# An image and text attention block on one core: layer norm interleaved, scaling while leaving PSUM, a new order of v's parts, and another load order

## The chip, the cores and the metric

The kernel runs on one core of a Trainium2 chip. The metric is device time in microseconds for one execution; 125.17 us is the median of three runs before the change. The engines are named as in the profile: PE (matrix multiplication; PEld is its weight load), DVE (vector), ACT (scalar, activation functions), POOL (GpSimd) and SP (which issues transfers). PE writes into PSUM, eight banks of accumulators; DVE and ACT read it, POOL works on SBUF alone. Each engine runs its own queue in order and waits for others by semaphores.

## What is computed

Two batches of 256 image tokens and 32 text tokens, width D = 1152, all in bfloat16:

```python
mod_i = (_silu(c) @ wmod_img).reshape(B, 6, 1, D)
mod_t = (_silu(c) @ wmod_txt).reshape(B, 6, 1, D)
hi = _layernorm(x_img, axis=-1) * (1 + sci) + shi
ht = _layernorm(x_txt, axis=-1) * (1 + sct) + sht
qkvi = hi @ wqkv_img
qkvt = ht @ wqkv_txt
...
scores = jnp.einsum('bqd,bkd->bqk', q, k) * D ** (-0.5)
p = _softmax(scores, axis=-1)
a = jnp.einsum('bqk,bkd->bqd', p, v)
...
out_i = x_img + gai * (ai @ wo_img)
out_t = x_txt + gat * (at @ wo_txt)
```

`shi`, `sci`, `gai` (shift, scale, gate) are the first three of the six parts of `mod_i`, and `sht`, `sct`, `gat` those of `mod_t`. q, k and v join the text and the image rows.

## The kernel before

The order of the work on every engine is written out by hand: instructions go into each queue in the order of the program. The 512 image tokens are four tiles of 128 (0 and 1 are batch 0, 2 and 3 batch 1), and D is nine blocks of 128 (`kt`). `hT_i` holds the normalised image tokens transposed: D on the partitions, in nine blocks, tokens along the free axis.

**Loads.** All big loads are in SP's queue, in program order: token tiles 0 and 1, then chunk 0 of the scale weight `w_sc_i` and of v's weight `w_v_i` (`load_pair`), token tiles 2 and 3, the chunks 1 to 3 of that pair, the text tokens, the shift weight `w_sh_i`, q's weight `w_q_i` in three thirds. `KC` cuts the nine blocks into chunks of 2, 2, 2 and 3. Later loads (in `load_w`, L76) are text shift `w_sh_t`, text scale `w_sc_t`, image k `w_k_i`, and on to the output weights. Whole weights share six buffers (`wpool`); a seventh weight waits until a buffer's last reader is done.

**First stage (L214 to L307).** For each tile: statistics in three chunks of 384 (`ln_stats`, L143), their aggregate (L145), a square root on ACT (L147), then reciprocal and normalisation on DVE (`ln_apply`, L151, L152); nine PE transposes into two PSUM tiles of five and four blocks (`x_transposes`, L161), which ACT copies into `hT_i` (L162). The scale is computed chunk by chunk on PE (`mod_scale`, L169; from PSUM by ACT, L179, or DVE, L177), and multiplied into `hT_i` in place (`apply_mod`: DVE L187, POOL L190 or L192, ACT L194 or L196). `v_part(i, half, ch)` (L208) adds chunk `ch` to the accumulator of one half of v's columns (512) of token tile `i`; seven such accumulators stay open in PSUM. PSUM has seven banks for all of this (`ps_mm`) and one (`ps_sm`) for the modulation. v uses the scaled but not yet shifted tokens; its remaining columns follow in `v_rest` (L296) and L303.

**Shift.** `mod_cols` (L169) with `w_sh_i` gives the image shift; DVE copies it to `mod_i` (L309), ACT to `shT32` (L310), and `apply_mod` adds it to `hT_i` in place. What the shift adds to v is one row for each batch, computed from `shT32` by `mod_rows` (L334), sent to memory (L344), broadcast back (`bvb`, L350), and added by `v_shift` (L354). 

**q, k and the text.** `qk_img` (L378) makes q, then k, column block by column block: the first group has three blocks of 128 columns, then one by one, nine matmuls each. Calls can be hooked in ahead of a group. `txt_rows_shift` and `txt_rows_scale` make the text modulation as rows: 36 matmuls (L334), out of PSUM (ACT L137 or DVE L338), two writes to memory each by POOL (L344); after the scale, four loads by POOL broadcast both to the text tokens' partitions (`mb_t`, L392). `txt_modulate` (L400, L401, DVE) multiplies and adds, `txt_transposes` (L406 PE, L407 ACT) makes `hT_t`, and only then come the text's q and k (L418), the scores, the softmax, the product with v and the outputs.

Of the kernel before, what the change touches and what calls it, by code (L numbers as in the profile page):

```python
# [8 lines left out]
ACT = mybir.ActivationFunctionType  # L9
# [5 lines left out]
def kernel(  # L15
# [14 lines left out]
    nc = tc.nc  # L30
    bf = mybir.dt.bfloat16
    f32 = mybir.dt.float32
    PSUM = bass.MemoryType.PSUM

    B, NI, D = x_img.shape
# [101 lines left out]
            nc.scalar.copy(out_ap, in_ap)  # L137
        evac_idx[0] += 1

    def ln_stats(x_ap, np_):  # L140
        stats = small.tile([P, NCH, 6], f32, tag="stats")
        for k in range(NCH):
            nc.vector.bn_stats(stats[0:np_, k, :], x_ap[:, k * CH:(k + 1) * CH])  # L143
        mv = small.tile([P, 2], f32, tag="mv")
        nc.vector.bn_aggr(mv[0:np_, :], stats[0:np_, :, :])  # L145
        rstd = small.tile([P, 1], f32, tag="rstd")
        nc.scalar.activation(rstd[0:np_, :], mv[0:np_, 1:2], ACT.Sqrt, bias=eps_t[0:np_, :])  # L147
        return mv, rstd

    def ln_apply(x_ap, np_, out_ap, mv, rstd):  # L150
        nc.vector.reciprocal(rstd[0:np_, :], rstd[0:np_, :])  # L151
        nc.vector.tensor_scalar(out_ap, x_ap, mv[0:np_, 0:1], rstd[0:np_, :], op0=ALU.subtract, op1=ALU.mult)  # L152

    xn_i = act.tile([P, NIT, D], bf, tag="A")
    hT_i = act.tile([P, KT, B * NI], bf, tag="Bt")

    def x_transposes(i):
        for (k0, k1) in ((0, 5), (5, KT)):
            tp = ps_mm.tile([P, 5, P], bf, tag="mm")
            for kt in range(k0, k1):  # L160
                nc.tensor.transpose(tp[:, kt - k0, :], xn_i[:, i, kt * P:(kt + 1) * P], ident[:])  # L161
            nc.scalar.copy(hT_i[:, k0:k1, i * P:(i + 1) * P], tp[:, 0:k1 - k0, :])  # L162

    mod_i = const.tile([P, 2 * KT, B], f32, name="mod_img")

    def mod_cols(wt, out_ps, j0, j1):
        for j in range(j0, j1):
# [34 lines left out]
    def v_part(i, half, ch):  # L202
        k0, k1 = KC[ch]
        if ch == 0:
            vacc[i, half] = ps_mm.tile([P, VW], f32, tag="mm", name=f"va{i}{half}")
        ps = vacc[i, half]
        for kt in range(k0, k1):
            nc.tensor.matmul(ps[:], lhsT=hT_i[:, kt, i * P:(i + 1) * P], rhs=w_v_i[:, kt, half * VW:(half + 1) * VW],  # L208
                             start=(kt == 0), stop=(kt == KT - 1))
# [5 lines left out]
    st = ln_stats(x_i[:, 0, :], P)
    ln_apply(x_i[:, 0, :], P, xn_i[:, 0, :], *st)
    x_transposes(0)
    st = ln_stats(x_i[:, 1, :], P)
    mod_scale(0, "act")
    ln_apply(x_i[:, 1, :], P, xn_i[:, 1, :], *st)  # L220
    for kt in range(*KC[0]):
        apply_mod(kt, 0, 1, False, 1)
    x_transposes(1)
    for half in range(2):
        v_part(0, half, 0)
    st = ln_stats(x_i[:, 2, :], P)
    for kt in range(*KC[0]):
        apply_mod(kt, 1, 2, False, 1)
    ln_apply(x_i[:, 2, :], P, xn_i[:, 2, :], *st)
    mod_scale(1, "act")  # L230
    for half in range(2):
        v_part(1, half, 0)
    for kt in range(*KC[1]):
        apply_mod(kt, 0, 2, False, 1)
    x_transposes(2)
    st = ln_stats(x_i[:, 3, :], P)
    for kt in range(*KC[0]):
        apply_mod(kt, 2, 3, False, 1)
    ln_apply(x_i[:, 3, :], P, xn_i[:, 3, :], *st)
# [3 lines left out]
    x_transposes(3)
    for half in range(2):
        v_part(2, half, 0)
    for kt in range(*KC[0]):
        apply_mod(kt, 3, 4, False, 1)
    for kt in range(*KC[1]):
        apply_mod(kt, 2, 4, False, 0)
    mod_scale(2, "dve")  # L250
    for n, kt in enumerate(range(*KC[2])):
        apply_mod(kt, 0, 2, False, n % 2)
        apply_mod(kt, 2, 4, False, (n + 1) % 2)
    v_part(3, 0, 0)
    for half in range(2):
        v_part(2, half, 1)
    v_part(3, 0, 1)
# [12 lines left out]


    xn_t = act.tile([NTT, D], bf)
    st_t = ln_stats(x_t[:, :], NTT)
    ln_apply(x_t[:, :], NTT, xn_t[:, :], *st_t)
    junk = small.tile([P, 1], f32, bufs=1)
    nc.scalar.activation(junk[:], eps_t[:], ACT.Exp)
# [25 lines left out]
    for kt in range(KT):  # L302
        nc.tensor.matmul(ps[:], lhsT=hT_i[:, kt, 3 * P:4 * P], rhs=w_v_i[:, kt, VW:NM], start=(kt == 0), stop=(kt == KT - 1))  # L303
    evac(v_i[:, 3, VW:NM], ps[:])


    mps = ps_sm.tile([P, KT, B], f32, tag="sm")  # L307
# [1 line left out]
    nc.vector.tensor_copy(mod_i[:, 0:KT, :], mps[:])  # L309
    nc.scalar.copy(shT32[:, :, 0:B], mps[:])  # L310
    for kt in range(KT):
        apply_mod(kt, 0, TPB, True, (0, 1, 2, 0, 2, 1, 0, 0, 2)[kt])
    v_rest(TPB, NIT)

    w_sh_t = load_w(wmod_txt, 0)
    w_sc_t = load_w(wmod_txt, D)
    w_k_i = load_w(wqkv_img, D, K3)
    w_q_t = load_w(wqkv_txt, 0)
    w_k_t = load_w(wqkv_txt, D)
    w_ga_i = load_w(wmod_img, 2 * D)  # L320
# [22 lines left out]
        for b in range(B):  # L343
            nc.gpsimd.dma_start(gsc[si, b, :].rearrange("(g j) -> g j", g=NGG), g_sb[b:P:32, :])  # L344

    for kt in range(KT):
        apply_mod(kt, TPB, NIT, True, (0, 1, 2, 0, 2, 1, 0, 0, 2)[kt])
    mod_rows(w_v_i, 4, lhs=shT32)
    for b in range(B):
        nc.gpsimd.dma_start(bvb[:, b, :], gsc[4, b, :].partition_broadcast(P))  # L350
# [34 lines left out]
    def txt_rows_shift():  # L385
        mod_rows(w_sh_t, 0)
# [4 lines left out]
            for b in range(B):  # L391
                nc.gpsimd.dma_start(mb_t[b * NT:(b + 1) * NT, k, :], gsc[k, b, :].partition_broadcast(NT))  # L392

    qk_img(w_q_i, 0, hooks={5: v_shift, 6: txt_rows_shift})
    txt_rows_scale()

    hT_t = act.tile([P, KT, NTT], bf)

# [7 lines left out]
            nc.tensor.transpose(tpt[:, kt, :], xn_t[:, kt * P:(kt + 1) * P], ident[0:NTT, 0:NTT])  # L406
        nc.scalar.copy(hT_t[:], tpt[:])  # L407
# [227 lines left out]
```

## Time and profile before

| what | value |
|---|---|
| runs shown | 124.64, 125.17, 125.85 us |
| the profiled execution, first to last instruction | 124.3 us |
| PE busy | 110.7 us (89%) |
| DVE, ACT, POOL busy | 55.5, 31.6, 21.2 us |
| bytes moved, mean rate | 41.63 MB, 335 GB/s |

The page cuts the span into 40 slices of 3.1 us and gives each engine's busy share in tenths (9 is 90% or more), the granted PE clock, and the busy share of the transfer engines:

```profile
PE   0057999999999999999999999899999999999980
DVE  0778624146862120923022621134445656636680
ACT  4544052133572211110031121133524500012000
POOL 4005225160055030302430000002151000000000
PEclk9999999999999999999999999999999999999999
DMA  4999999999999999999999999999999997120231
```

PE starts in the third slice and is then busy to the end. The transfer engines are busy from the second slice to about 102 us. A row of the timeline gives start, length, engine, line, operation, the tile written and the tiles read, and the count of merged instructions; in square brackets stands the engine's idle time before it and what ended that. Matmuls overlap, so the length of a group is more than the sum of its steps; a step is the distance from one start to the next. A few matmul records are missing from the trace. In the chain of waits each piece has its start, its length and its line.

### The profile page before, as it was taken

The numbers are of one execution on the slowest core, as the hardware profiler recorded it, in microseconds if no ns is written. First come the engines' busy times: TensorE is split into PE (matmuls) and PEld (weight loads), VectorE is DVE, ScalarE is ACT, GpSimd is POOL, SyncE is SP. The second block draws the span as 40 slices with busy tenths as digits, with TensorE's granted clock in tenths as the row PEclk, the third lists the DMA queues.
The fourth block names the chain that finished last, engine by engine and source line by source line (L and its number), as shares of the span: only waits on it lengthen the run. The fifth ranks groups of instructions, "written<-read, shape, count | busy, mean of one in ns | idle before, by whom it ended". The sixth has DMA issues, their size and how long they took to land.

```text
span 124.3 us, 2647 instructions
## 1 busy us (share of the span) xinstructions
PE 110.7 (89%) x1126; PEld 65.8 (53%) x1134; DVE 55.5 (45%) x131; ACT 31.6 (25%) x72; POOL 21.2 (17%) x53
## 2 busy tenths in 40 slices
PE   0057999999999999999999999899999999999980
PEld 0044554546684444445444448777656555657650
DVE  0778624146862120923022621134445656636680
ACT  4544052133572211110031121133524500012000
POOL 4005225160055030302430000002151000000000
PEclk9999999999999999999999999999999999999999
DMA  4999999999999999999999999999999997120231
GB/s 107 267 348 376 377 383 350 348 414 413 408 406 413 397 414 422 406 406 412 404 383 402 381 409 411 407 411 405 411 405 417 371 411 299 61 95 0 100 96 49
DMA packets 22728, 41.63 MB, mean 335 GB/s; under 512 B 1148, under 2 KB 6428, under 8 KB 22716
## 3 DMA queue, kind: packets, MB, share of 16 engines
q1 hardware_dynamic: 21776, 39.74, 85.1%
q0 software_dynamic: 768, 1.64, 3.4%
q8 instruction: 9, 0.15, 0.4%
q10 hardware_dynamic: 171, 0.08, 0.2%
q14 instruction: 4, 0.02, 0.0%
HBM read 40.11 MB, written 1.35 MB: 333 GB/s over the span
## 4 chain that ended last, share of the span: by engine, by line
PE 85%; DVE 6%; ACT 4%; DMA 2%; issue 2%
PE qkps L378 28%; PE ps L568 13%; PE va L208 10%; PE gps L334 5%; PE ps L418 4%; PE aps L500 4%; PE sps L438 4%; PE mps L169 3%; ACT hT_i L162 2%; PE tp L161 2%; PE ps L587 2%; DMA c<-in_c_dram 2%; PE ps L515 2%; PE ps L296 2%; PE ps L303 2%
## 5 line engine op out<-in xcount | busy, mean ns | idle before, releaser
L378 PE MATMUL qkps<-hT_i,t 128*128 128x512 bf16 x157 | 35.4, 379 | 0.3
L378 PEld LDWEIGHTS <-t 128*128 128x128 bf16 x162 | 15.5, 98 | 18.9 <-issue 0.7
L568 PE MATMUL ps<-t,aT 128*128 128x384 bf16 (+2 forms) x117 | 18.1, 314 | 0.0
L208 PE MATMUL va<-w_v_i,hT_i 128*128 128x512 bf16 x60 | 16.0, 408 | 0.5 <-issue 0.2
L568 PEld LDWEIGHTS <-aT 128*128 128x128 bf16 x117 | 10.9, 98 | 6.8 <-issue 0.5
L571 DVE SCALAR_TENSOR_TENSOR tmp<-ps,rs,gb 128x384 bf16<-128x384 f32 (+2 forms) x13 | 7.6, 586 | 6.9 <-PE ps L568 6.9
L344 POOL DMA_DIRECT2D mod_scratch<-g_sb x8 | 4.8, 596 | 34.3 <-DVE g_sb L135 22.5
L208 PEld LDWEIGHTS <-hT_i 128*128 128x128 bf16 x63 | 6.2, 103 | 6.9 <-issue 1.5
L161 PE MATMUL tp<-ident,xn_i 128*128 128x128 bf16 x36 | 4.1, 287 | 5.4 <-DVE xn_i L152 5.4
L192 POOL TENSOR_SCALAR hT_i<-hT_i,mod_img 128x128 bf16<-128x128 bf16 (+1 forms) x14 | 6.1, 449 | 15.0 <-ACT mod_img L179 6.2
L362 DVE TENSOR_SCALAR qkT<-qkps 128x512 bf16<-128x512 f32 x5 | 3.4, 687 | 9.1 <-PE qkps L378 9.1
L137 ACT CAST qkT<-qkps 128x512 bf16<-128x512 f32 x5 | 2.8, 586 | 16.0 <-PE qkps L378 16.0
L161 PEld LDWEIGHTS <-xn_i 128*128 128x128 bf16 x36 | 3.3, 133 | 6.6 <-DVE xn_i L152 6.1
L135 DVE CAST qkT<-qkps 128x512 bf16<-128x512 f32 x4 | 2.8, 688 | 8.3 <-PE qkps L378 8.3
L162 ACT COPY hT_i<-tp 128x640 bf16<-128x640 bf16 (+1 forms) x8 | 4.7, 642 | 6.7 <-PE tp L161 6.7
L143 DVE BATCH_NORM_STATS2 stats<-x_i 128x6 f32<-128x384 bf16 x12 | 5.9, 546 | 0.0
L500 PE MATMUL aps<-pT,v_i 128*128 128x288 bf16 x36 | 5.4, 287 | 0.3 <-ACT pT L489 0.3
L418 PE MATMUL ps<-hT_t,t 128*128 128x64 bf16 x162 | 5.0, 193 | 0.5 <-issue 0.5
L418 PEld LDWEIGHTS <-t 128*128 128x128 bf16 x162 | 4.9, 98 | 0.9 <-issue 0.6
L364 ACT ACTIVATE qkT<-qkps 128x512 bf16<-128x512 f32 x4 | 2.3, 596 | 11.5 <-PE qkps L378 11.5
L334 PE MATMUL gps<-t,sT 128*32 128x288 bf16 x144 | 5.1, 287 | 0.0
L187 DVE TENSOR_SCALAR hT_i<-hT_i,mod_img 128x256 bf16<-128x256 bf16 x14 | 4.3, 368 | 1.5 <-ACT hT_i L162 1.3
(108 smaller groups left out, 119.0 us busy)
## 6 DMA issues: line engine op xcount, KB each, us to landing
t<-in_wmod_txt_dram SPq DMA_DIRECT2D x3, 2592.0 KB, 24.2
t<-in_wqkv_txt_dram SPq DMA_DIRECT2D x3, 2592.0 KB, 20.8
t<-in_wmod_img_dram SPq DMA_DIRECT2D x2, 2592.0 KB, 18.7
t<-in_wqkv_img_dram SPq DMA_DIRECT2D x6, 864.0 KB, 15.8
t<-in_wo_img_dram SPq DMA_DIRECT2D x1, 2592.0 KB, 22.1
t<-in_wo_txt_dram SPq DMA_DIRECT2D x1, 2592.0 KB, 24.3
w_sc_i<-in_wmod_img_dram SPq DMA_DIRECT2D x3, 576.0 KB, 7.8
w_v_i<-in_wqkv_img_dram SPq DMA_DIRECT2D x3, 576.0 KB, 7.9
```

The costliest lines, as they stand in the source:

```text
L143: nc.vector.bn_stats(stats[0:np_, k, :], x_ap[:, k * CH:(k + 1) * CH])
L161: nc.tensor.transpose(tp[:, kt - k0, :], xn_i[:, i, kt * P:(kt + 1) * P], ident[:])
L162: nc.scalar.copy(hT_i[:, k0:k1, i * P:(i + 1) * P], tp[:, 0:k1 - k0, :])
L192: nc.gpsimd.tensor_scalar(sl, sl, ap, 0.0, op0=ALU.mult, op1=ALU.add)
L208: nc.tensor.matmul(ps[:], lhsT=hT_i[:, kt, i * P:(i + 1) * P], rhs=w_v_i[:, kt, half * VW:(half + 1) * VW], start=(kt == 0), stop=(kt == K ...
L334: nc.tensor.matmul(gps[32 * g:32 * g + 32, :], lhsT=lhs[:, kt, :], rhs=w_blk[:, kt, g * VC:(g + 1) * VC], start=(kt == 0), stop=(kt == KT ...
L378: nc.tensor.matmul(pss[j - j0][:], lhsT=wq[:, kt, j * P:(j + 1) * P], rhs=hT_i[:, kt, :], start=(kt == 0), stop=(kt == KT - 1))
L418: nc.tensor.matmul(ps[:, j - j0, :], lhsT=wq[:, kt, j * P:(j + 1) * P], rhs=hT_t[:, kt, :], start=(kt == 0), stop=(kt == KT - 1))
L438: nc.tensor.matmul(sps[:], lhsT=qkT[:, ft, b, q0:q0 + P], rhs=qkT[:, KT + ft, b, :], start=(ft == 0), stop=(ft == KT - 1))
L500: nc.tensor.matmul(aps[:], lhsT=v_i[:, b * TPB + kj, dt * P:(dt + 1) * P], rhs=pTs[b][:, kj, :], start=(kj == 0), stop=False)
L568: nc.tensor.matmul(ps[:, 0:cw], lhsT=aT[:, dt, t0:t0 + P], rhs=w_o_i[:, dt, cs], start=(dt == 0), stop=(dt == KT - 1))
L571: nc.vector.scalar_tensor_tensor(tmp[:, 0:cw], ps[:, 0:cw], rsum[(b, qi)][:], gb[:, b, cs], op0=ALU.mult, op1=ALU.mult)
```

## The change

Five edits of order, and one of how the scale is applied.

1. `ln_stats` is split. The first statistics chunk of the next tile goes into DVE's queue ahead of the reciprocal and the normalisation of the tile before it; its other two chunks follow behind.
2. `x_transposes` only transposes. Its PSUM tile is emptied in parts: the first two blocks (four for tile 3) by ACT with the scale in the same instruction (`evac_scaled`), the others as plain copies (`evac_plain`). The steps of `apply_mod` for chunk 0 are gone, and that of chunk 1 for tile 3.
3. v's parts run in another order, with tile 0 and tile 1 chunk 0 together after tile 1's transposes.
4. `v_rest` for batch 1 moves ahead of the shift, and the shift is added to both batches block by block.
5. `w_k_i` is loaded ahead of `w_sh_t` and `w_sc_t`. The text modulation rows move out of the q pass into the k pass, behind its first three columns; `txt_modulate` and `txt_transposes` stand behind the k pass.

```diff
+    def evac_scaled(i, tps, n):
+        for kt in range(n):
+            nc.scalar.activation(hT_i[:, kt, i * P:(i + 1) * P], tps[0][:, kt, :], ACT.Identity,
+                                 scale=mod_i[:, KT + kt, i // TPB:i // TPB + 1])
+
+    def evac_plain(i, tps, n):
+        nc.scalar.copy(hT_i[:, n:5, i * P:(i + 1) * P], tps[0][:, n:5, :])
+        nc.scalar.copy(hT_i[:, 5:KT, i * P:(i + 1) * P], tps[1][:, 0:KT - 5, :])
...
+    def ln_next(i, first):
+        if first:
+            lns[i] = ln_stats(x_i[:, i, :], P, 0, 1)
+        else:
+            ln_stats(x_i[:, i, :], P, 1, NCH, lns[i])
+            lns[i] = ln_std(lns[i], P)
...
+    ln_next(0, True)
+    ln_next(0, False)
+    ln_next(1, True)
+    ln_out(0)
+    tps = x_transposes(0)
+    evac_plain(0, tps, 2)
+    ln_next(1, False)
+    ln_next(2, True)
+    ln_out(1)
     mod_scale(0, "act")
+    evac_scaled(0, tps, 2)
+    tps = x_transposes(1)
+    evac_scaled(1, tps, 2)
+    ln_next(2, False)
+    ln_next(3, True)
+    ln_out(2)
+    evac_plain(1, tps, 2)
+    for i in range(2):
+        for half in range(2):
+            v_part(i, half, 0)
+    tps = x_transposes(2)
+    evac_scaled(2, tps, 2)
+    ln_next(3, False)
+    ln_out(3)
     mod_scale(1, "act")
+    evac_plain(2, tps, 2)
     for kt in range(*KC[1]):
         apply_mod(kt, 0, 2, False, 1)
+    for kt in range(*KC[1]):
+        apply_mod(kt, 2, 3, False, 0)
+    v_part(2, 0, 0)
+    tps = x_transposes(3)
+    evac_scaled(3, tps, 4)
+    evac_plain(3, tps, 4)
     for i in range(2):
         for half in range(2):
             v_part(i, half, 1)
+    v_part(2, 0, 1)
     mod_scale(2, "dve")
+    for kt in range(*KC[2]):
+        apply_mod(kt, 0, 2, False, 0)
+        apply_mod(kt, 2, 4, False, 1)
+    for (i, half) in ((2, 1), (3, 0)):
+        for ch in range(2):
+            v_part(i, half, ch)
...
+    v_rest(TPB, NIT)
...
     for kt in range(KT):
-        apply_mod(kt, 0, TPB, True, (0, 1, 2, 0, 2, 1, 0, 0, 2)[kt])
-    v_rest(TPB, NIT)
-
+        apply_mod(kt, 0, TPB, True, (0, 1, 2, 0, 2, 0, 1, 0, 2)[kt])
+        apply_mod(kt, TPB, NIT, True, (2, 0, 1, 0, 2, 0, 0, 1, 2)[kt])
+
+    w_k_i = load_w(wqkv_img, D, K3)
     w_sh_t = load_w(wmod_txt, 0)
     w_sc_t = load_w(wmod_txt, D)
-    w_k_i = load_w(wqkv_img, D, K3)
...
-    for kt in range(KT):
-        apply_mod(kt, TPB, NIT, True, (0, 1, 2, 0, 2, 1, 0, 0, 2)[kt])
...
-    qk_img(w_q_i, 0, hooks={5: v_shift, 6: txt_rows_shift})
-    txt_rows_scale()
+    qk_img(w_q_i, 0, hooks={5: v_shift})
...
+    def txt_rows():
+        txt_rows_shift()
+        txt_rows_scale()
+
-    qk_img(w_k_i, 1, hooks={5: txt_modulate, 8: txt_transposes})
+    qk_img(w_k_i, 1, hooks={3: txt_rows})
+    txt_modulate()
+    txt_transposes()
```

The last argument of `apply_mod` names the engine: 0 is DVE, 1 POOL, 2 ACT. In the diff above the removed lines of the first stage are left out; they stand in the listing of the kernel before.

More of the change, by code (lines that the diff above doesn't have):

```diff
@@ L138, in evac, with ln_stats, ln_std @@
         evac_idx[0] += 1
-    def ln_stats(x_ap, np_):
-        stats = small.tile([P, NCH, 6], f32, tag="stats")
-        for k in range(NCH):
+    def ln_stats(x_ap, np_, k0, k1, stats=None):
+        if stats is None:
+            stats = small.tile([P, NCH, 6], f32, tag="stats")
+        for k in range(k0, k1):
             nc.vector.bn_stats(stats[0:np_, k, :], x_ap[:, k * CH:(k + 1) * CH])
+        return stats
+    def ln_std(stats, np_):
         mv = small.tile([P, 2], f32, tag="mv")
@@ L155 @@
     hT_i = act.tile([P, KT, B * NI], bf, tag="Bt")
+    mod_i = const.tile([P, 2 * KT, B], f32, name="mod_img")
     def x_transposes(i):
+        tps = []
         for (k0, k1) in ((0, 5), (5, KT)):
@@ L161, in x_transposes @@
                 nc.tensor.transpose(tp[:, kt - k0, :], xn_i[:, i, kt * P:(kt + 1) * P], ident[:])
-            nc.scalar.copy(hT_i[:, k0:k1, i * P:(i + 1) * P], tp[:, 0:k1 - k0, :])
-    mod_i = const.tile([P, 2 * KT, B], f32, name="mod_img")
+            tps.append(tp)
+        return tps
+    def evac_scaled(i, tps, n):
[5 more added lines that the diff above has]
+        nc.scalar.copy(hT_i[:, 5:KT, i * P:(i + 1) * P], tps[1][:, 0:KT - 5, :])
     def mod_cols(wt, out_ps, j0, j1):
@@ L214, with ln_out @@
     silu_c()
[L215 to L218, printed above, removed]
-    mod_scale(0, "act")
[L220 to L229, printed above, removed]
+    lns = {}
+    def ln_next(i, first):
[4 more added lines that the diff above has]
+            lns[i] = ln_std(lns[i], P)
+    def ln_out(i):
+        ln_apply(x_i[:, i, :], P, xn_i[:, i, :], *lns[i])
+    ln_next(0, True)
[7 more added lines that the diff above has]
+    ln_out(1)
+    mod_scale(0, "act")
+    evac_scaled(0, tps, 2)
[12 more added lines that the diff above has]
+    ln_out(3)
     mod_scale(1, "act")
-    for half in range(2):
-        v_part(1, half, 0)
+    evac_plain(2, tps, 2)
     for kt in range(*KC[1]):
         apply_mod(kt, 0, 2, False, 1)
[L235 to L239, printed above, removed]
+    for kt in range(*KC[1]):
[4 more added lines that the diff above has]
+    evac_plain(3, tps, 4)
     for i in range(2):
@@ L242 @@
             v_part(i, half, 1)
[L243 to L249, printed above, removed]
-    mod_scale(2, "dve")
[L251 to L257, printed above, removed]
+    v_part(2, 0, 1)
+    mod_scale(2, "dve")
+    for kt in range(*KC[2]):
[4 more added lines that the diff above has]
+            v_part(i, half, ch)
     v_i = act.tile([P, NIT, D], bf, tag="A")
@@ L272 @@
     xn_t = act.tile([NTT, D], bf)
-    st_t = ln_stats(x_t[:, :], NTT)
+    st_t = ln_std(ln_stats(x_t[:, :], NTT, 0, NCH), NTT)
     ln_apply(x_t[:, :], NTT, xn_t[:, :], *st_t)
```

## The prediction

> **What bounds the kernel now.** I read the page first: who is busy, and which engine carries the chain of waits.
>
> ```profile
> PE 110.7 (89%) x1126; PEld 65.8 (53%) x1134; DVE 55.5 (45%) x131; ACT 31.6 (25%) x72; POOL 21.2 (17%) x53
> ...
> PE 85%; DVE 6%; ACT 4%; DMA 2%; issue 2%
> ```
>
> PE carries 85% of the chain and from 10 us on hardly stops, so an edit counts only where it makes PE wait or stop waiting. No weight load is on the chain; what idle time there is to win lies in the first 20 us. So next came the timeline of the start (start, length, engine, line, tile, count), and the transfer that brings token tile 2 (issued at 3.34; 6.6 us to landing, so in memory at 9.94).
>
> ```profile
> 3.34 1.19 SPq L87 DMA_DIRECT2D x_i<-in_x_img_dram  x2
> 9.32 0.62 DVE L152 TENSOR_SCALAR xn_i<-x_i,mv,rstd 128x1152 bf16<-128x1152 bf16 x1
> 9.94 1.48 DVE L143 BATCH_NORM_STATS2 stats<-x_i 128x6 f32<-128x384 bf16 x3
> 10.00 1.14 PE L161 MATMUL tp<-ident,xn_i 128*128 128x128 bf16 x9 [1.44 <-DVE xn_i L152]
> 10.93 1.91 PE L208 MATMUL va<-w_v_i,hT_i 128*128 128x512 bf16 x4
> 15.77 1.89 PE L208 MATMUL va<-w_v_i,hT_i 128*128 128x512 bf16 x8
> 17.84 0.68 PE L161 MATMUL tp<-ident,xn_i 128*128 128x128 bf16 x9 [0.18 <-DVE xn_i L152]
> ```
> ```profile
> x_i<-in_x_img_dram SPq DMA_DIRECT2D x1, 288.0 KB, 6.6
> ```
>
> See two things. DVE normalises tile 1 (9.32) before it touches tile 2, and PE's transposes follow at 10.00. And the same 128x512 matmul steps by 0.427 us at 10.93 (four until 12.64) but by 0.217 from 15.77 (eight in 1.73): PE is at half speed until about 15.7, though the page's clock row shows full all along. Last, the text modulation's round trip, and the end of the image-bias stage:
>
> ```profile
> 35.08 0.18 DVE L309 COPY mod_img<-mps 128x18 f32<-128x18 f32 x1 [0.91 <-PE mps L169]
> 35.35 0.17 ACT L310 CAST shT<-mps 128x18 bf16<-128x18 f32 x1 [0.80 <-DVE mod_img L309]
> 36.00 1.29 PE L334 MATMUL gps<-w_v_i,shT 128*32 128x288 bf16 x36
> ```
> ```profile
> 56.13 1.29 PE L334 MATMUL gps<-t,sT 128*32 128x288 bf16 x36
> 57.47 0.46 DVE L338 TENSOR_SCALAR g_sb<-gps 128x288 bf16<-128x288 f32 x1 [0.54 <-PE gps L334]
> 58.21 1.10 POOL L344 DMA_DIRECT2D mod_scratch<-g_sb  x2 [6.06 <-DVE g_sb L338]
> 63.69 0.98 POOL L392 DMA_DIRECT2D mb_t<-mod_scratch  x2 [3.35 <-DMA mod_scratch<-g_sb]
> 69.34 0.75 DVE L400 TENSOR_TENSOR xn_t<-xn_t,mb_t 64x1152 bf16<-64x1152 bf16 x1 [3.33 <-DMA mb_t<-mod_scratch]
> 70.13 0.75 DVE L401 TENSOR_TENSOR xn_t<-xn_t,mb_t 64x1152 bf16<-64x1152 bf16 x1
> 72.99 0.43 PE L406 MATMUL tpt<-ident,xn_t 64*128 64x64 bf16 x9
> 73.46 0.64 ACT L407 COPY hT_t<-tpt 128x576 bf16<-128x576 bf16 x1 [1.72 <-PE tpt L406]
> ```
>
> From the end of the scale rows' matmuls (57.42) to a modulated text tile (70.88) is 13.46 us: rows to memory, broadcast back, two DVE steps. PE comes for it at 72.99, so it is hidden with 2.1 us to spare.
>
> **Part 1, layer norm.** DVE's order becomes: first statistics chunk of tile 2, then reciprocal and normalisation of tile 1. That chunk needs tile 2, in memory at 9.94; DVE, free since about 8.2, waits, and tile 1 queues behind it. A chunk costs 0.47 (three in 1.40 in the chain), reciprocal to normalisation 0.20, normalisation 0.62, the step to PE 0.05: 9.94+0.47+0.20+0.62+0.05, so tile 1's transposes start at 11.30, not 10.00: +1.3. Tile 0's chunk lies in the 0.35 us in which DVE waits for ACT's square root (5.78 to 6.13) and delays its normalisation by 0.1, hidden behind the same wait.
>
> **Part 2, v's parts and scaled evacuation.** From tile 1's transposes to the third modulation block (23.41) PE does the same work in both kernels: 27 transposes at 0.057 (nine in 0.51 from 17.84), 36 matmuls at 0.217, 36 two-column matmuls at 0.026: 1.54+7.81+0.92 = 10.27 at full speed. Before, this took 13.41. The excess of 3.14 is 8 matmuls at +0.21 and 18 transposes at +0.046 at half speed (2.51) and two waits (17.50 to 17.84, 18.79 to 19.07: 0.63). After: nine transposes at 0.103 from 11.30 to 12.23, then eight matmuls in a row at 0.427 to 15.65, when the speed changes as before: excess 2.09. Tile 2's transposes end at 16.2, and now ACT is in the way: its two scaled evacuations come before tile 3's square root in its queue. The profile has no 128-column ACTIVATE with a pointer; bounds are 0.17 (128x4) and 0.50 (128x256 from SBUF); I take 0.35, nearer the wide one. Two: 16.9, so PE, out of work after the second modulation block at 16.65, waits 0.3, does two matmuls (to 17.4), and waits for tile 3: square root 0.30, reciprocal 0.20, normalisation 0.58 after 16.9 give 18.0: 0.6. By the bounds 0.5 to 1.5 for both. Third block at 11.30+10.27+2.09+0.9 = 24.56 against 23.41: **+1.15** (0.7 to 1.8). POOL loses eight 0.41 us steps that PE waited for nowhere on the chain; the ten ACT steps and four tile copies end near 20.6, their last users start at 22: hidden.
>
> The Trainium skill (TensorE: Matmul & The Clock Gate, Part 1) says the clock is halved until a free-running window of about 3.4 us was busy, and its table for kernel authors warns of PE gaps over 3 us, against a change that stretches the gap before tile 1 from 1.6 to 2.8 us. No row here shows the window's phase. Estimated from that page, a run dense from 11.3 could reach full speed between 14.7 and 18.1, moving the sum by -0.5 to +1.2.
>
> **Part 3, v's rest ahead of the shift.** v_rest for batch 1 (18 matmuls, 1.03 in the chain, 35.04 to 36.07) used to run while the shift went from PSUM over DVE (35.08) to ACT (until 35.52) to the bias rows. Moved ahead, the rows start about 0.5 after the shift's matmuls with PE idle: **+0.5** (0.4 to 0.6). The 18 shift applications have 1.7 us until the first q matmul and then 0.65 per k: enough, from eight DVE steps in 2.30.
>
> **Part 4, text rows inside the k pass, w_k_i first.** Matmuls are the same number. But the scale rows now end after three k columns and both blocks of rows, with six columns left: 54 matmuls at 0.217 (72 from 57.41 to 73.06) are 11.7. POOL's two shift writes go first (1.15, ready 0.45 before the scale block ends) and free POOL at +0.7, when the scale rows arrive (+0.8): no delay. The round trip stays 13.46, so PE waits 13.5-11.7 = 1.8 before the text transposes. Behind that wait stand all text q and k matmuls and the scores. And the transposes' copy (L407, 0.64 and two handovers of 0.04), which ran under the last k column, is exposed: 0.7. Together **+2.5**. Nearest rows bound the two transfers: 4.5 to 5.5 for a row write, 4.8 to 6.0 for a broadcast, so 1.9 to 4.1.
>
> The Trainium skill (DMA: Bandwidth & Descriptors, Anatomy of one DMA) fits a GpSimd-issued transfer as 2.0 us plus bytes over 436 GB/s. That would make each leg about 2.1, an estimate; the trace has 4.9 to 5.1 in a full stream, and I go by the trace. By the page the rows would be in time and the sum 1.8 less.
>
> The load order gains nothing that shows: PE waits for no image weight at either pass. By issue and landing, 43.4 (text shift), 51.3 (text scale) and 57.8 (last third of k) become k, text shift, text scale, each needed later (q ends near 56.5, rows at 62). SP stands later for one buffer (text v, now after the rows near 64, before issued at 61.94); the stream ahead covers it, and text v has 4.0 us spare (84.8 landed, 88.77 used); uncovered it costs what exceeds that, plus PE's own delay.
>
> **The sum.** 1.15+0.5+2.5 = +4.15 on a span of 124.3: 128.45. The median of the runs shown, 125.17, lies 0.87 above that span (launch edges and other executions, which differ by 1.2 among themselves), so 129.3.
>
> **Rivals.** (a) The rows come in time, legs of 4.0 or less, because another stretch of the stream is quieter. For: the outputs at the end land in 1.5. Against: the DMA row is full from 6 to 104 us. PE's 1.8 goes, 0.7 stays: 127.5. (b) The pauses before and inside the text transposes (1.8 and 0.7, little between) halve PE's speed again. For: the start shows half speed after idling. Against: no pause of up to 0.7 us did it after 16 us. The start lost 2.5 to half speed; the text matmuls (5.0 us in all) could lose some two thirds of that, 1.7: 131. (c) Not slower: the first stage's excess was not clock but matmuls fed late by POOL's L192 steps, and scaled evacuation removes all 3.14. For: POOL's idle time before L192 ends on ACT's copies. Against: transposes, which take nothing from POOL, also halve their step at 15.7. Then the third block starts at 21.6 in place of 23.41, and with the rows at their lower bound (1.9) the sum is -1.85+0.5+1.9 = +0.55: 125.7. It decides from a third block at about 22.3 on, and is faster by over 1% only before 19.8. That the change doesn't do what it says is excluded by the code: the orders are written out.
>
> **Numbers.** Forecast 0.72, (a) 0.10, (b) 0.10, (c) 0.08. The forecast's bounds sum to +3.0 and +6.5, 128.2 to 131.7; all upper ends at once are unlikely, and (a) and (b) belong inside: 127.1 to 131.3. One per cent, what a measurement can tell here, is 1.25: slower (over 126.4) 0.91; within 0.06; faster 0.03, the last two from (c) alone and its tail.
>
> **What would show it.** Part 1: tile 1's normalisation starting right after a chunk that begins at tile 2's landing. Part 2: third block at 24 to 25, ACT's scaled evacuations ahead of the square root. Part 3: PE waiting for the shift's cast. Part 4: PE waiting near 76 us for the text tile, about 1.8, then 0.7 for the copy. Wrong it is if tile 1 is transposed by 10.3, or the text tile is ready when the k pass ends.

## The result and the profile after

The kernel after takes 131.85 us (median of 4 executions, 131.60 to 132.63), against 125.17 before: a ratio of 1.054, with an interval of 1.049 to 1.059. It is slower by 6.7 us. The forecast was 129.3, the range up to 131.3.

The profiled execution has a span of 129.9 (131.93 us in all), against 124.3. The page of the kernel after, busy time and the chain of waits:

```profile
PE 112.5 (87%) x1134; PEld 67.4 (52%) x1134; DVE 55.4 (43%) x131; ACT 33.4 (26%) x82; POOL 18.2 (14%) x45
...
PEclk9999999999999999999999999599999999999998
...
PE 73%; DMA 13%; DVE 5%; SPq 2%; ACT 2%; issue 2%; POOL 1%; DVEq 0%; POOLq 0%; ACTq 0%
```

PE was 85% of the chain and is 73% now; transfers went from 2% to 13%. The chain now waits for transfers in two places, for the landing of a token tile and for the text rows. And the clock row has a 5 in slice 26 (81.2 to 84.4 us), where it had none. The timeline of the start of the kernel after, with the lines that answer to those of before:

```profile
10.31 0.56 DVE L144 BATCH_NORM_STATS2 stats<-x_i 128x6 f32<-128x384 bf16 x1 [2.46 <-DMA x_i<-in_x_img_dram]
10.97 0.58 DVE L156 TENSOR_SCALAR xn_i<-x_i,mv,rstd 128x1152 bf16<-128x1152 bf16 x1
11.61 1.14 PE L168 MATMUL tp<-ident,xn_i 128*128 128x128 bf16 x9 [2.79 <-DVE xn_i L156]
12.54 3.62 PE L224 MATMUL va<-w_v_i,hT_i 128*128 128x512 bf16 x8
16.70 0.63 ACT L174 ACTIVATE hT_i<-tp,mod_img 128x128 bf16<-128x128 bf16 x2 [2.68 <-PE tp L168]
16.72 0.59 PE L185 MATMUL mps<-sT,w_sc_i 128*128 128x2 bf16 x18
18.53 0.68 PE L168 MATMUL tp<-ident,xn_i 128*128 128x128 bf16 x9 [0.76 <-DVE xn_i L156]
```

DVE stands still for 2.46 us until tile 2 lands, takes the one chunk, and only then normalises tile 1 (10.97), whose transposes start at 11.61. All eight v matmuls behind them run at half speed (12.54 to 15.95, 0.427 a step). The trace's clock records have the change to full speed at 16.50, within tile 2's transposes; the 18 two-column matmuls at 16.72 are the first group that runs wholly at full speed.

The shift and the text rows, down to the first text matmuls, timeline of the kernel after:

```profile
38.05 0.17 ACT L341 CAST shT<-mps 128x18 bf16<-128x18 f32 x1 [1.53 <-DVE mod_img L340]
38.28 1.29 PE L365 MATMUL gps<-w_v_i,shT 128*32 128x288 bf16 x36 [0.54 <-ACT shT L341]
...
64.94 2.27 POOL L375 DMA_DIRECT2D mod_scratch<-g_sb  x4 [17.05 <-ACT g_sb L137]
65.24 11.83 PE L407 MATMUL qkps<-hT_i,t 128*128 128x512 bf16 x54
70.44 2.21 POOL L421 DMA_DIRECT2D mb_t<-mod_scratch  x4 [3.23 <-DMA mod_scratch<-g_sb]
77.65 0.75 DVE L428 TENSOR_TENSOR xn_t<-xn_t,mb_t 64x1152 bf16<-64x1152 bf16 x1 [1.80 <-DMA mb_t<-mod_scratch]
79.24 0.43 PE L434 MATMUL tpt<-ident,xn_t 64*128 64x64 bf16 x9 [2.18 <-DVE xn_t L429]
79.71 0.64 ACT L435 COPY hT_t<-tpt 128x576 bf16<-128x576 bf16 x1 [2.02 <-PE tpt L434]
80.40 6.43 PE L452 MATMUL ps<-hT_t,t 128*128 128x64 bf16 x162 [0.73 <-ACT hT_t L435]
```

From the chains of waits, first of the kernel before, then of the kernel after: the third modulation block, the first q matmuls, and the text matmuls, for the kernel after with the two transfers ahead of them:

```profile
23.57 0.66 PE mps L169 x27
37.28 0.32 PE qkps L378
75.47 4.35 PE ps L418 x149
79.82 0.52 issue
80.34 0.54 PE ps L418 x13
```
```profile
25.27 0.66 PE mps L185 x27
39.57 23.42 PE qkps L407 x108
64.94 5.22 DMA mod_scratch<-g_sb
72.16 5.40 DMA mb_t<-mod_scratch
80.40 6.43 PE ps L452 x162
```

PE waits 0.54 for the shift's cast, and 2.18 and 0.73 for the text tile. The text q and k matmuls (L452; L418 before) took 4.35, an idle row of 0.52 and 0.54, together 5.41, in the kernel before; they take 6.43 now. By the chains of both kernels the loss stands in four places. The third modulation block starts at 25.27 against 23.57: +1.70. From there to the start of q it is 14.30 against 13.71, the 0.54 wait among it: +0.59. From the start of q to the text matmuls it is 40.83 against 38.19: +2.64. The text matmuls: +1.02. The sum is +5.95; behind them nothing changes (40.39 us to the last output step in both), and the last transfers end 0.35 sooner, which leaves 5.6 on the span.

### The profile page after: what moved, and what is told of

Same layout as the page of the kernel before. It is cut to its first block, busy times and chain, and to the rows that moved or that the text cites. A ratio compares the mean times of both kernels' runs of the same rounds, so it can differ in the third digit from the quotient of the medians.

```text
span 129.9 us, 2657 instructions
## 1 busy us (share of the span) xinstructions
PE 112.5 (87%) x1134; PEld 67.4 (52%) x1134; DVE 55.4 (43%) x131; ACT 33.4 (26%) x82; POOL 18.2 (14%) x45
## 3 DMA queue, kind: packets, MB, share of 16 engines
q1 hardware_dynamic: 21776, 39.74, 81.2%
## 4 chain that ended last, share of the span: by engine, by line
PE 73%; DMA 13%; DVE 5%; SPq 2%; ACT 2%; issue 2%; POOL 1%; DVEq 0%; POOLq 0%; ACTq 0%
PE qkps L407 18%; PE ps L602 13%; PE va L224 11%; DMA x_i<-in_x_img_dram 5%; PE ps L452 5%; DMA mb_t<-mod_scratch 4%; DMA mod_scratch<-g_sb 4%; PE gps L365 4%; PE aps L534 4%; PE sps L472 4%; PE mps L185 2%; PE tp L168 2%; PE ps L621 2%; PE ps L549 2%; PE ps L326 2%
## 5 line engine op out<-in xcount | busy, mean ns | idle before, releaser
L407 PEld LDWEIGHTS <-t 128*128 128x128 bf16 x162 | 15.7, 98 | 19.1 <-issue 0.5
L135 DVE CAST qkT<-qkps 128x512 bf16<-128x512 f32 x5 | 3.4, 690 | 14.2 <-PE qkps L407 14.2
L452 PE MATMUL ps<-hT_t,t 128*128 128x64 bf16 x162 | 6.4, 212 | 0.7 <-ACT hT_t L435 0.7
L452 PEld LDWEIGHTS <-t 128*128 128x128 bf16 x162 | 6.4, 111 | 0.8 <-issue 0.7
L393 ACT ACTIVATE qkT<-qkps 128x512 bf16<-128x512 f32 x5 | 2.9, 597 | 14.3 <-PE qkps L407 14.3
L137 ACT CAST qkT<-qkps 128x512 bf16<-128x512 f32 x4 | 2.3, 586 | 16.3 <-PE qkps L407 16.3
L208 POOL TENSOR_SCALAR hT_i<-hT_i,mod_img 128x256 bf16<-128x256 bf16 x6 | 3.1, 529 | 20.0 <-ACT mod_img L195 13.6
L391 DVE TENSOR_SCALAR qkT<-qkps 128x512 bf16<-128x512 f32 x4 | 2.7, 687 | 6.1 <-PE qkps L407 6.1
L135 DVE CAST aT<-aps 128x288 bf16<-128x288 f32 x9 | 3.7, 453 | 2.6 <-PE aps L540 2.6
L472 PE MATMUL sps<-qkT 128*128 128x288 bf16 x36 | 4.8, 287 | 0.0
```

The source lines that it names most:

```text
L135: nc.vector.tensor_copy(out_ap, in_ap)
L407: nc.tensor.matmul(pss[j - j0][:], lhsT=wq[:, kt, j * P:(j + 1) * P], rhs=hT_i[:, kt, :], start=(kt == 0), stop=(kt == KT - 1))
L452: nc.tensor.matmul(ps[:, j - j0, :], lhsT=wq[:, kt, j * P:(j + 1) * P], rhs=hT_t[:, kt, :], start=(kt == 0), stop=(kt == KT - 1))
L472: nc.tensor.matmul(sps[:], lhsT=qkT[:, ft, b, q0:q0 + P], rhs=qkT[:, KT + ft, b, :], start=(ft == 0), stop=(ft == KT - 1))
```

## Experiments

Labels e1 to e16; the kernel before ran beside each and gave medians of 125.16 to 125.60. The parts are numbered as in the prediction; the first experiments take them apart.

**Text rows alone.** The kernel before with part 4.

```diff
+    w_k_i = load_w(wqkv_img, D, K3)
     w_sh_t = load_w(wmod_txt, 0)
     w_sc_t = load_w(wmod_txt, D)
-    w_k_i = load_w(wqkv_img, D, K3)
...
-    qk_img(w_q_i, 0, hooks={5: v_shift, 6: txt_rows_shift})
-    txt_rows_scale()
+    qk_img(w_q_i, 0, hooks={5: v_shift})
...
-    qk_img(w_k_i, 1, hooks={5: txt_modulate, 8: txt_transposes})
+    qk_img(w_k_i, 1, hooks={3: txt_rows})
+    txt_modulate()
+    txt_transposes()
```

> The kernel before with part 4 alone: image k's weight loaded first, text rows behind the first three k columns, text modulation and transposes behind the k pass. Theory (the text rows' round trip is not hidden, and the pause halves PE's speed for a while): PE waits about 2 us before the text transposes and 0.7 for their copy, and the text matmuls take 6.4 in place of 5.4, so 3.6 more than before, about 128.8. Rival (the first stage made the change's loss and the wait only shows up because PE came late or early to it): PE finds the text tile ready or waits under 0.5, 125.2 to 126. Open: time outside the span was 0.9 before and 2.0 after; if part 4 carries that, 1.2 more, 130.0.

Measured: 129.96 (129.18 to 130.02), ratio 1.036 (1.031 to 1.041): +4.6. Its timeline:

```profile
76.22 0.43 PE L405 MATMUL tpt<-ident,xn_t 64*128 64x64 bf16 x9 [2.64 <-DVE xn_t L400]
77.38 6.55 PE L423 MATMUL ps<-hT_t,t 128*128 128x64 bf16 x162 [0.73 <-ACT hT_t L406]
```

The waits are those of the kernel after, 2.64 before the text transposes and 0.73 for the copy, and the text matmuls take 6.55. From the start of q to the text matmuls the chain has 41.29 against 38.19 before, so between the two profiled executions 3.1 is lost there and 1.1 in the text matmuls. This one part is two thirds of the whole loss.

**Text rows undone in the kernel after.** The same diff backwards.

> The changed kernel with part 4 undone: load order, text rows and their hooks as before. Theory: the 2.6 of waiting and the 1.0 of half speed go, first stage and shift stay: 131.85 less 3.6, about 128.2 (127.0 if the time outside the span goes too); PE at full speed from about 16.5 to the end. Rival (the first stage is the loss): 130.5 or more.

Measured: 128.55 (126.99 to 129.17), ratio 1.022 (1.014 to 1.030): 3.3 less than after. There is no text wait, and the text matmuls take 5.26, an idle row of 0.36 among it. But here PE slowed down elsewhere. Three stretches; a row has the stretch and its length, the busy time (and instructions) of PE, PEld, DVE, ACT and POOL, then the mean granted clock (1.00 is full), and the share and rate of the transfers:

```profile
34.00:38.00 4.00, 3.46 (x123) 3.25 (x122) 2.05 (x7) 2.46 (x8) 1.20 (x3) 1.00 1.04 405
38.40:41.70 3.30, 3.08 (x8) 1.22 (x8) 0.98 (x4) 0.95 (x3) 1.91 (x4) 0.50 1.05 409
42.00:46.00 4.00, 4.00 (x21) 1.80 (x19) 0.26 (x1) 0.48 (x1) 0.64 (x2) 1.00 1.04 406
```

The clock is half at the start of q, behind 81 two-column matmuls and the wait for the cast: eight matmuls of 512 columns in 3.3 us. One execution of the four had a mean granted clock of 0.998 and took 126.99; two at 0.987 took 128.53 and 128.56. So the 3.3 understates what the text rows cost: here a loss elsewhere stood in their place.

**Layer norm's place undone in the kernel after.**

```diff
-    ln_next(2, True)
     ln_out(1)
+    ln_next(2, True)
```

> The changed kernel with one pair of calls swapped: tile 1 is normalised before the first statistics chunk of tile 2. Theory (the chunk waits for tile 2's landing, and tile 1 behind it): tile 1's transposes start at 9.6 to 10.0 in place of 11.6, the third modulation block at 23.4 to 24.0 in place of 25.3, total 1.3 to 1.7 less, about 130.3. Rival (PE waits for the slow clock and for later tiles in any case): third block at 25 or later, total within 0.4 of 131.85.

Measured: 129.91 (129.46 to 130.22), ratio 1.037 (1.032 to 1.041): 1.9 less than after. Its timeline:

```profile
9.78 1.14 PE L168 MATMUL tp<-ident,xn_i 128*128 128x128 bf16 x9 [1.23 <-DVE xn_i L156]
10.72 3.20 PE L224 MATMUL va<-w_v_i,hT_i 128*128 128x512 bf16 x8
```

Two swapped lines bring tile 1's transposes back from 11.61 to 9.78, and the third block from 25.27 to 22.80. Text waits (2.16 and 0.73) and text matmuls (6.46) stay as after.

**Shift order alone.** The kernel before with part 3.

```diff
+    v_rest(TPB, NIT)
     mps = ps_sm.tile([P, KT, B], f32, tag="sm")
...
-    v_rest(TPB, NIT)
```

> The kernel before with the third part of the change alone: v_rest for batch 1 ahead of the shift, and the shift added to both batches block by block. Theory: PE waits some 0.5 us for the cast of the shift before the bias rows, and nothing else changes: 125.8 to 126.0, ratio 1.004. If the pause, coming after 36 matmuls of two columns, also lets the clock halve at the start of q (as it did in two runs, 38.36 to 41.77), another 1.4 to 2.0 in those executions: up to 127.5. Rival: the shift applications now stand together ahead of q and hide the pause, or the pause is made up before the row round trip ends: within 0.2 of the kernel before.

Measured: 125.94 (125.31 to 127.76), ratio 1.004 (1.000 to 1.008). The timeline shows the wait:

```profile
35.68 1.29 PE L335 MATMUL gps<-w_v_i,shT 128*32 128x288 bf16 x36 [0.53 <-ACT shT L311]
```

The wait is there in full: from the third modulation block to the start of q the chain has 14.30, as in the kernel after, where the kernel before has 13.71. The median is 0.34 above the kernel before's. Two of the ten executions took 126.84 and 126.85 at a mean granted clock of 0.986, where the profiled one has 0.997; the place of that loss is not recorded for them. It would fit the half speed at the start of q that e2 shows, but that is not shown.

**Three parts undone.** The kernel after with all three of these put back; what remains is the scaling while leaving PSUM, the order of v's parts, and the other tiles' statistics.

> The changed kernel with three things undone: part 4, the place of tile 2's first chunk, and v's rest for batch 1 (back behind the shift's matmuls). What stays is the interleaving otherwise, the scaled evacuation and v's new order. Theory: 131.85 less 3.6, 1.5 and 0.5 is 126.2, or 125.0 if the time outside the span goes with part 4; that is within 1% of before. Rival (v's new order and the scaled evacuation themselves cost): 127.5 or more, with the third block at 25 us.

Measured: 125.13 (124.74 to 125.68), ratio 0.998 (0.995 to 1.001). The rest of the change, taken together, is worth nothing that can be measured. The three parts by themselves give 4.6 (e1), 1.9 (e3) and 0.3 (e10, with an interval from 0 to 1.0), 6.8 in all, and the loss is 6.7.

**Load order.** One line of part 4, alone in the kernel before:

```diff
+    w_k_i = load_w(wqkv_img, D, K3)
     w_sh_t = load_w(wmod_txt, 0)
     w_sc_t = load_w(wmod_txt, D)
-    w_k_i = load_w(wqkv_img, D, K3)
```

> The kernel before with one line moved: w_k_i is loaded ahead of the text shift and scale weights. Theory: neutral, as the prediction has it, 125.2 to 125.5, no wait of PE for any of the three weights. Rival: the text shift rows, which the kernel before has in the q pass, now wait for their weight, since k's 2.65 MB go first (about 7 us of the stream): the rows move back, PE waits up to 2 us in the q pass and the text rows come late, 126 to 128.

Measured: 129.32 (129.19 to 129.97), ratio 1.032 (1.028 to 1.037). The first expectation fell. The timeline:

```profile
50.73 1.95 PE L334 MATMUL gps<-t,sT 128*32 128x288 bf16 x36 [2.69 <-DMA t<-in_wmod_txt_dram]
52.61 6.97 PE L378 MATMUL qkps<-hT_i,t 128*128 128x512 bf16 x26
```

PE waits 2.69 for the text shift weight. The rows behind the wait take 1.95 where they took 1.29 in the kernel before, and the 26 matmuls after them 6.97, where 26 steps of 0.217 are 5.64: after the wait the clock is half (0.53 on average from 51.0 to 54.5). Together that is 4.7 in this execution, whose third block came 1.0 sooner than in the profiled one of the kernel before (22.40 against 23.41 by the timelines); the median is 3.7 higher. So the load order is dear with the rows in the q pass. With the rows in the k pass it should cost nothing; the reverse edit in the kernel after:

> The kernel after with w_k_i loaded behind the text shift and scale weights again, as in the kernel before; all else as after. In the kernel before the new load order alone cost 4 us, since its rows stand in the q pass. Theory: with the rows in the k pass both orders are in time, so it is neutral as predicted: 131.6 to 132.2. Rival A: the new order is needed, PE waits for k's weight at the head of the k pass without it: 132.5 to 135. Rival B: the new order delays the row transfers, and the old one is faster by 0.5 or more: below 131.3.

Measured: 131.88 (131.22 to 132.22), as after. There the order is indeed neutral.

**The text matmuls.** They lost 1.0 that the forecast had at nothing. Rival (b) had said half speed after the pause, and the windows of the kernel after agree:

```profile
81.40:84.70 3.30, 3.30 (x68) 3.30 (x65) 0.56 (x1) 0.33 (x1) 0.00 (x0) 0.50 1.05 411
```

So I filled the pause with eight matmuls whose result nobody reads:

```diff
+    fps = ps_mm.tile([P, B * NI], f32, tag="mm", name="fillps")
+    for _ in range(8):
+        nc.tensor.matmul(fps[:], lhsT=w_k_i[:, 0, 0:P], rhs=hT_i[:, 0, :], start=True, stop=True)
     txt_modulate()
```

> The changed kernel with 8 extra 128x512 matmuls (1.73 us) behind the k pass, into a PSUM tile that nobody reads, in the 2.2 us in which PE waits for the text tile. The waiting stays. Theory (the pause halves PE's speed for one 3.4 us stretch): the text matmuls take 5.4 in place of 6.4 and the clock stays full after 17 us; total 0.3 to 1.0 less, about 131.1. Rival (the small text matmuls themselves let the speed drop, or the drop costs nothing): 6.4 again, or 131.85 within 0.3.

Measured: 133.01 (131.27 to 133.19), ratio 1.058 (1.049 to 1.066): no gain, 1.2 more than after. The clock stayed full in the text matmuls of the profiled execution (131.27), and yet, in its chain:

```profile
79.38 4.24 PE ps L455 x140
83.62 1.74 issue
85.36 0.81 PE ps L455 x22
```

They take 6.79, with a stop of 1.74 in which PE waits for nothing that the profile shows. (The other three executions had a mean granted clock of 0.985 to 0.987 instead of 0.996; where, is not recorded.) The same stop shows in the next experiment, whose edit is meant to shorten the pause: the rows stand at the head of the k pass.

```diff
-    qk_img(w_k_i, 1, hooks={3: txt_rows})
+    qk_img(w_k_i, 1, hooks={0: txt_rows})
```

> The changed kernel with the text rows ahead of the k pass's first group in place of behind its third column, 5.8 us earlier. Theory (the rows' round trip of 13.5 us against the matmuls left is what PE waits for): 17.5 us of matmuls now cover it, the 1.9 to 2.2 of waiting goes, the copy's 0.7 stays; total 2 to 3 less, 129 to 130. Rival (the transfers run slower in this stretch and PE waits in any case): the text transposes still start over 1 us behind the last k matmul, 131 or more.

Measured: 129.66 (129.42 to 130.71), ratio 1.036 (1.029 to 1.042): 2.2 less than after. Its timeline:

```profile
77.73 0.43 PE L434 MATMUL tpt<-ident,xn_t 64*128 64x64 bf16 x9 [0.28 <-DVE xn_t L429]
78.89 4.48 PE L452 MATMUL ps<-hT_t,t 128*128 128x64 bf16 x148 [0.73 <-ACT hT_t L435]
84.93 0.58 PE L452 MATMUL ps<-hT_t,t 128*128 128x64 bf16 x14 [1.56 <-issue]
```

The wait before the text transposes falls from 2.18 to 0.28; the stop stays. It comes after 148 of the 162 matmuls, in e7 after 140, eight sooner, as eight more stood ahead: it sits at a fixed place in PE's count of instructions. The transfer queues of the page hold nine packets of 16 KB of an instruction queue (0.15 MB), and one of them lies there: 82.62 to 83.55 in e8, 83.05 to 84.02 in e7, with PE going on 1.3 to 1.4 us after its end. In the kernel after one lies at 83.96 to 84.92, so PE could go on at 86.3, which is when the half-speed matmuls got to the 148th. To test it I moved the place, with 40 two-column matmuls of the identity at the start, where PE has nothing to do:

```diff
     silu_c()
+    wps = ps_mm.tile([P, P], f32, tag="mm", name="tinyps")
+    for _ in range(40):
+        nc.tensor.matmul(wps[:, 0:2], lhsT=ident[:], rhs=ident[:, 0:2], start=True, stop=True)
```

> The kernel after with 40 two-column matmuls of the identity put behind the transposition of c, where PE has nothing else to do. They take about 1 us together, too little to warm PE, but they shift by 40 matmuls (80 instructions, with the weight loads) the place at which PE's next piece of instructions has to be fetched. In the kernels after, with the rows late, with plain layer norm and with the filled pause, one 16 KB packet of PE's instruction queue lands 3.6 to 3.7 us after the start of the text q and k matmuls, and PE stands still before the same matmul (the 148th of 162; the 140th where 8 were added ahead) for 0.5 to 1.7 us. Theory 'fetch': what the text matmuls lost is this fetch, so it moves out of them: no idle row of 'issue' among the text matmuls; they take about 4.7 us at a full clock or 6.2 to 6.4 where the clock halves after the pause (in place of 6.4 to 6.8 in both); the total falls by 0.3 to 1.7 from 131.85, to 130.2 to 131.5. Rival 'clock': the loss is half speed after the pause alone, so the text matmuls take 6.4 again and the total stays within 0.3 of 131.85. Rival 'start': the 40 matmuls hinder or help the first stage, to be seen at the third modulation block (25.27 in the kernel after).

Measured: 132.36 (131.61 to 133.16), ratio 1.055 (1.049 to 1.062), the total not lower. (The profiled execution, 132.86, was at half speed at the start of q too, from 36.93 to 40.34.) The packet has moved to 88.83, behind the text matmuls, but in its chain and its windows:

```profile
81.38 6.38 PE ps L455 x162
```
```profile
81.40:84.70 3.30, 3.30 (x63) 3.30 (x63) 0.24 (x1) 0.00 (x0) 0.00 (x0) 0.50 1.04 411
```

Now half speed alone makes 6.38. Each edit alone had let the other cause show: the filled pause the stop, the moved place the half speed. Both edits together:

> The kernel after with both additions: 8 matmuls of 512 columns whose result nobody reads in the text pause (which kept the clock full there), and the 40 two-column matmuls at the start (which moved the instruction fetch out of the text matmuls). Alone, each left the text matmuls at 6.4 to 6.8 us. Theory 'two covers': the half speed after the pause and the late fetch each cost 1.7 to 2 us in the text matmuls and lie over one another, so only both together show: text matmuls 4.7 us, no row of issue in them, and the time from the start of the transposes of the text tile to the end of the text matmuls 5.9 in place of 7.6. The total is then 130.2 to 130.8 where no other stretch is halved, up to 132 where the start of q is. Rival: a third cause keeps them at 6.4 or more.

Measured: 129.81 (129.53 to 130.50), ratio 1.037 (1.030 to 1.043): 2.0 less than after, below the expected 130.2. Its timeline:

```profile
78.38 0.43 PE L437 MATMUL tpt<-ident,xn_t 64*128 64x64 bf16 x9 [0.79 <-DVE xn_t L432]
79.53 4.88 PE L458 MATMUL ps<-hT_t,t 128*128 128x64 bf16 x162 [0.73 <-ACT hT_t L438]
```

The text matmuls take 4.88 in one piece, 1.55 less than after. The span of this execution is 2.4 shorter than that of the kernel after (127.5 against 129.9): its third block also came 1.2 sooner (24.06 against 25.27), and from the start of q to the text matmuls it took 0.34 more. And the moved place with the rows at the head of k:

> The kernel after with the text rows at the head of the k pass (129.66, text matmuls at a full clock with an idle row of 1.56 for instructions, 6.62 in all) and with the 40 two-column matmuls at the start. Theory 'fetch': with the boundary elsewhere the text matmuls take 4.7, and the total falls by 1.9 to 127.5 to 127.9 in executions with a full clock; an execution that halves the clock at the text pause keeps 6.4 and stays near 129.4. Rival: the fetch is not the cause, 129.4 to 129.9 and 6.4 or more at a full clock.

Measured: 128.27 (127.64 to 128.97), ratio 1.023 (1.016 to 1.029), 1.4 less than e8 where 1.9 was expected; one execution of four lies in the expected 127.5 to 127.9. The profiled one began late (third block at 25.17, against 23.96 in e8). The timeline, with a granted clock of 1.00 there:

```profile
78.42 4.88 PE L455 MATMUL ps<-hT_t,t 128*128 128x64 bf16 x162 [0.73 <-ACT hT_t L438]
```

So the stop costs 1.7 at a full clock (6.62 to 4.88). In the kernel before, where no pause stands ahead, it should cost less:

> The kernel before with the 40 two-column matmuls at the start. In the kernel before the text matmuls take 5.41, with an idle row of 0.52 for instructions after 149 of them. Theory 'fetch': without a pause the fetch costs some 0.5 to 0.7; text matmuls 4.7, total 124.6 to 125.1, if the 40 matmuls (about 1 us, where PE waits for the first tile) leave the first stage as it is. Rival: the fetch is hidden or moves to another dense place, 125.2 to 125.7.

Measured: 124.28 (123.89 to 125.28), ratio 0.992 (0.989 to 0.995): 0.9 faster than before, with 4.72 of text matmuls in the chain in place of 5.41. The line of its chain:

```profile
73.89 4.72 PE ps L421 x162
```

The gain is 0.2 more than that. In this execution full speed came at 12.26 and the third block at 21.99, earlier than in the three profiled executions of before, e1 and e10 (22.37 to 23.57); whether the 40 matmuls bring that too is not shown.

**A faster version.** Forty matmuls of 128 columns to keep PE busy in the first stage (30 behind the transposition of c, 10 behind the first modulation block), in the kernel before, and in e4:

```diff
+    def warm(n):
+        wps = ps_mm.tile([P, P], f32, tag="mm", name="warmps")
+        for _ in range(n):
+            nc.tensor.matmul(wps[:], lhsT=ident[:], rhs=ident[:], start=True, stop=True)
+
     silu_c()
+    warm(30)
...
     mod_scale(0, "act")
+    warm(10)
```

> The kernel before with 40 extra 128x128 matmuls of the identity into a PSUM tile that nobody reads: 30 behind the transposition of c, 10 behind the first modulation block, in time in which PE idles. Theory (the first stage's excess is half speed, set by how idle PE was, and the change pays it later and longer): the first v matmuls step by 0.217 in place of 0.427, the third modulation block starts at 21.0 to 22.0 in every execution (22.2 and 23.4 in the two profiles of this order so far), total 0.7 to 1.7 less than before, about 124. Rival (matmuls are fed late by POOL and DVE): the block stays at 22.2 or later and the total within 0.4 of before.

> The kernel of e4 with the same 40 extra matmuls. Theory: first v matmuls at full speed, third block at 21.5 to 22.3 (e4: 23.3), 0.7 to 1.5 less than e4's 125.1, about 124; tile 3's square root behind the scaled evacuations then limits it. Rival: 124.8 or more. If it is under e5 the change's v order and scaled evacuation gain something once PE is fast; if above, they cost.

Measured: 124.05 (123.81 to 125.48), ratio 0.991 (0.987 to 0.994), and 123.83 (123.52 to 123.93), ratio 0.988 (0.983 to 0.992). Both beat both kernels, by about one per cent of the kernel before. In both the text matmuls take 4.72 without a stop, and of the 1.4 and 1.6 us that they gain, e15's edit alone, which moves that place too, gives 0.9; what the warmth gives beyond it was not separated. Nor did the warmth last in the profiled execution of e5, the slowest of its ten (125.48): the clock was full from 6.95, half again from 13.77 to 17.18, and the third block came at 23.60, not by 22.0 as expected. With ten more ahead of c's transposition:

> The change without its three dear parts (layer norm place, v's rest, text rows), and with PE kept warm in the first stage by 50 matmuls of 128 columns whose result nobody reads (10 ahead of c's transposition, 30 behind it, 10 behind the first modulation block); 40 of them gave 123.83. Theory: the start is limited by the window of the clock: full from about 10 us in place of 11.6, third block by 21.4, total 123.3 to 123.8. Rival: the ten matmuls ahead of c delay c's transposition and the first block, total 123.9 to 124.5.

Measured: 123.94 (123.83 to 124.31), ratio 0.988 (0.984 to 0.992). The expected 123.3 to 123.8 was missed: the third block of the profiled execution came at 22.54, later than the 21.80 of e6, although its clock was full from 6.62 on, against 11.62 in e6. So an early full clock alone doesn't set the third block; what held it was not followed.

## Why the prediction was right and wrong

It was right in sign, and for each of its four parts a wait that it named is in the trace. It gave 129.3 and the time is 131.85. Of the 2.55, 1.45 is the span (5.6 against 4.15) and 1.1 the step from the span to the time. Two steps failed: the sum put the text matmuls at nothing, and they took 1.02 more (rival (b), below); and it took 0.87 from span to time, where the profiled execution of the kernel after has 2.03. The terms of the four parts were together 0.8 too small, and the end of the kernel came 0.35 sooner.

**Part 1, right.** Tile 1 behind a chunk that begins at tile 2's landing, as foreseen; 11.61 for 11.30, since tile 2 landed at 10.28, not 9.94. In the kernels with this order the start varies from 10.70 to 11.62 between executions.

**Part 2, the size off.** Third block +1.70 for +1.15. 0.31 is the later start. The rest is the sentence "when the speed changes as before": I took the change to full speed at 15.7 from one execution. It came at 16.50 in the kernel after and at 14.47 in e2, with the same first stage; in the kernel before's first stage it came at 15.74 in the profile, and at 12.85 in e1. Over the profiled executions the third block of the chain came at 22.37 to 23.57 with the first stage of before (before, e1, e10) and at 23.96 to 25.27 with that of after (eight kernels), so another pair of profiles could have given anything from +0.4 to +2.9; how near +1.70 comes to +1.15 is in part luck. Of the two waits behind ACT only the second came, with a row of 0.76 (0.91 in steps, as the sum counts) for 0.9 in all; ACT's scaled pair took 0.63 for the 0.70 assumed. The Trainium skill (TensorE: Matmul & The Clock Gate, Part 1) says that the change depends on a free-running window of 3.4 us. These runs agree: in the clock records of the kernel after half speed lasts 3.413 us, and full speed before it 64.853, nineteen times that. In the eight profiled executions with this first stage, full speed came 3.41 to 5.75 us after the start of tile 1's transposes. I gave the window a sentence and kept the row's one value in the sum.

**Part 3, right.** +0.54 for +0.5 by the wait, and +0.59 from the third block to q, in the kernel after and alone (e10), where the median moved by 0.3.

**Part 4, right as a wait.** 2.18 for 1.8, 0.73 for 0.7, +2.64 for +2.5. The legs took 5.22 and 5.40; the estimate of 2.1 from the Trainium skill (DMA: Bandwidth & Descriptors, Anatomy of one DMA) is not borne out in this stream, and rival (a) fell. "The load order gains nothing" held for the kernel after (e16), while the same line alone costs 3.7 us in the kernel before (e11): the prediction's reason, that each weight is needed later, holds only with the rows moved.

**Rival (b), the step that failed.** The sum has no term for the text matmuls, so it left them as they were in the kernel before. I gave 0.10 to half speed after the pauses, because no wait of up to 0.7 had done it. The new pause was 2.18 and 0.73 with 0.45 of work between them, and it did it in the profiled executions of after, e1, e3, e9 and e16. Half speed costs 1.5 (6.38 in e9 against 4.88 in e13), near the 1.7 that the rival gave. The net is 1.0, as the 0.52 stop of the kernel before vanishes under it. Nor would another phase of the clock have helped: at a full clock the stop for instructions grows to 1.56 and 1.74 (e8, e7). In the kernel after one execution had a granted clock of 1.0 all along and took 131.77 all the same. This second cause was in no rival, though its idle row of 0.52 stood in the profile of before. With it, +1.0 was due in either case and the sum would have been 5.15.

**Rival (c)** fell: the third block was later, not at 21.6. With POOL's steps for the first chunk gone, the eight v matmuls still stepped by 0.427 until the clock record turned full, so those slow steps were the clock's and not POOL's. And e4 shows that the scaled evacuation and v's new order bring nothing together; they were not taken apart.

**The last step, from span to time.** I added 0.87, the distance of the median from the span of the profiled execution. But what lies outside a span is 1.7 to 2.2 in the executions of all these kernels: 124.3 went with 126.13, 123.3 with 125.17, and 129.9 with 131.93. So the profiled execution of before was one of the slowest, about 1 us over its median, and the 0.87 mixed a constant near 1.9 with that. Its first stage fits that: full speed at 15.74 and the third block at 23.57, where e1 and e10, with the same first stage, had 12.85 and 13.87, and 22.37 and 22.67. The forecast added its steps to a late start.

## What to carry to other kernels

A reorder that lets work start "sooner" in a strict queue puts whatever stands behind it at the mercy of its operand: tile 1 waited for tile 2's landing (1.9 us for two swapped lines). A round trip through memory, here of about 14 us, needs that much of other PE work after it is sent; moving its start by some columns turned cover into a wait, and the pause was paid a second time in what ran right after it. When one cause is removed and nothing moves, look for a second one of the same size under it, and remove both before either is dismissed.

## What the runs showed that was not expected

A stop of PE goes with the packets of its instruction queue. It showed at one place of the instruction count, moved with it (e7), left the text matmuls when it was moved by 40 matmuls (e9, e13, e14, e15), and cost 0.23 to 0.52 where the matmuls ran up to it without a pause (before, e2, e4, e10, e11) and 1.56 to 1.74 behind a pause at a full clock (e8, e7). From the start of the text matmuls to the packet it is 2.2 to 2.5 us without a pause and 3.6 to 3.7 behind one. Why the packet comes later there stays open.

Half speed came back after less idling than I had assumed: after pauses of 2.18 and 0.73, in e11 behind a wait of 2.69, and in e2, e8 and e9 for 3.4 us at the start of q, behind two-column matmuls and a wait of 0.54. The Trainium skill (TensorE: Matmul & The Clock Gate, HAM oscillation) warns of gaps over about 3.4 us. Here shorter ones did it, the longest of them 2.69.
